# Keys and values of one batch kept for both parities, and position tables from one pattern

## The chip, the cores and the metric

One core of one Trainium2 chip runs the kernel. The metric is the device time of one execution in microseconds (us). The kernel before takes 676.55 us, the median of three runs (675.37 to 677.56). PE is TensorE, DVE VectorE, ACT ScalarE, POOL GpSimd, SP SyncE, which issues nearly all transfers.

## The reference

Attention with sinks and a sliding window, then a mixing block of low rank and a feed-forward net:

```
B, H, S, D = 4, 8, 768, 64        # n_sink = 4, window = 128
keep = (pos_k < n_sink) | ((pos_q - pos_k >= 0) & (pos_q - pos_k < window))
a = softmax(where(keep, q @ k.T / sqrt(D), -1e9));  x = a @ v    # heads joined: (B, S, 512)
h = x.transpose(0, 2, 1) @ U @ V                                 # U: 768x32, V: 32x768, float64
u = x + h.transpose(0, 2, 1)
out = u + relu(u @ w_ch1) @ w_ch2                                # 512 -> 2048 -> 512, float64
```

q, k and v are float32; U, V and both weight matrices arrive as float64 and are narrowed on the chip (`narrow`, seven or so small operations for each block on DVE, ACT and POOL).

## The kernel before

**Work and order.** Every operation is a step of a planner (`Plan`, line 293). A step has a modelled duration on each engine that could do it, the steps that it must follow and a priority. `order` runs a greedy list schedule forward and backward for 40 rounds, keeps the one of least modelled cost, and the steps are then written out in that order: each engine executes its own list in order, SP's list of transfers too. Operations ahead of the main program (lines 1620 to 1650) are outside the plan; the narrowing of U, V and the first weight block is in the plan, without its loads, so the plan takes these as present at its start.

**Start.** Eight products of zeros wake PE. SP loads the two scalars (n_sink and window), keys of two pairs, U, V in two parts and a weight block. `Masks.__init__` (line 173) builds four tables of distances, 128 x 132 each, with POOL's iota and some fifteen DVE operations. `values` (line 155) turns the scalars into a flag with five small DVE operations; all engines load the flag and branch (line 1651). `Masks.fill` (line 209) turns the tables into additive masks, before DVE's own branch. The main program is `Fast`; `General` is for other scalars and does not run.

**Attention of batch 0.** 768 positions are split into two parities of 64-row blocks, "half 0" and "half 1". `attention_halves` (line 859) does all four pairs of heads for half 0, then for half 1; for each, `load` (line 715) fetches queries, keys (`kp`, 128 x 792) and values (`vp`, 128 x 768), then come scores (PE, line 744), a fold and a masked reduction on DVE (lines 752, 757), the exponential on ACT (line 760), scaling, transposes (line 799), and value products (line 827). `kp`, `qp` and `vp` are rings of NRAW = 3 tiles: a load waits until the third load before it has been read. Queries are loaded by half; keys and values are the same for both halves and loaded twice. The other batches do both halves at once, in the shadow of the feed-forward net.

**Mixing and feed-forward.** When both halves are done, `mix_end` forms the mixed input, and `ffn` (line 1024) runs batch 0 (first product at line 1046). `weights` (line 679) narrows pairs of weight blocks into NSLOT = 3 slots of two tiles (`w0` to `w5`, 8 KB of each partition). `join` (`nt`) is scratch of the narrowing, cleared once on POOL (line 1647) and first needed by line 142. `shrink` and `stage` reuse rings and weight tiles later.

Of the kernel before, what the change touches and what calls it, by code (L numbers as in the profile page):

```python
# [21 lines left out]
P = 128  # L22
B, H, S, D = 4, 8, 768, 64
NB = S // P
# [145 lines left out]
class Masks:  # L170


    def __init__(self, nc, pool):
        self.nc, self.work = nc, pool
        raw = pool.tile([P, 4, SW], I32, name="mask")
        self.m = m = f32(raw)
        self.now, self.past = (pool.tile([P, G], I32, name=x) for x in ("now", "past"))
        two = lambda x: x.rearrange("p k (s c) -> p k s c", s=2)
        nc.gpsimd.iota(two(raw[:, 0:2, :P]), [[0, 2], [G, 2], [-1, G]], base=0, channel_multiplier=1)
        nc.gpsimd.iota(two(raw[:, 2:4, NS:]), [[0, 2], [-G, 2], [-1, G]], base=G, channel_multiplier=1)  # L180
        nc.gpsimd.iota(raw[:, 0:2, P:], [[4 * P, 2], [-1, NS]], base=0, channel_multiplier=1)
        nc.gpsimd.iota(raw[:, 2:4, :NS], [[4 * P, 2], [-1, NS]], base=G, channel_multiplier=1)
        cix = pool.tile([P, 4, NS], I32, name="m_cix")
        nc.gpsimd.iota(cix, [[0, 4], [1, NS]], base=0, channel_multiplier=0)
        self.cix = f32(cix)
        flat = lambda x: x.rearrange("p a b -> p (a b)")
        nc.vector.tensor_copy(flat(self.m), flat(raw))
        nc.vector.tensor_copy(self.cix, cix)
        v = nc.vector
        lo, hi = slice(0, G), slice(G, P)  # L190
        v.tensor_scalar(flat(m[hi]), flat(m[hi]), -float(G), None, ALU.add)
        far = pool.tile([P, 2, G], F32, name="m_far")
        back = m[:, 1, :G]
        v.tensor_scalar(self.now, back, 0.0, None, ALU.is_ge)
        v.tensor_scalar(self.past, back, 0.0, None, ALU.is_lt)
        v.tensor_scalar(far[:, 1], back, 0.0, float(P), ALU.is_lt, ALU.mult)
        v.tensor_scalar(far[lo, 0], back[lo], 0.0, FAR, ALU.is_lt, ALU.mult)
        fold = lambda x: x.unsqueeze(1)
        for at in (m[:, 0:2, :G], m[:, 2:4, NS + G:]):
            v.tensor_tensor(at[hi], at[hi], far[hi, 1].unsqueeze(1).broadcast_to([G, 2, G]), ALU.add)  # L200
            v.tensor_tensor(at[lo], at[lo], far[lo], ALU.add)
        nc.gpsimd.memset(m[lo, 0, G:P], FAR)
        sinks = m[lo, 0, P:]
        v.tensor_scalar(far[lo, 0, :NS], sinks, 0.0, FAR, ALU.is_lt, ALU.mult)
        v.tensor_tensor(sinks, sinks, far[lo, 0, :NS], ALU.add)
        for sinks in (m[hi, 0, P:], m[hi, 2, :NS]):
            v.tensor_scalar(sinks, sinks, float(P), None, ALU.add)

    def fill(self, ns, w):
        nc, m = self.nc, self.m  # L210
        ck = self.work.tile([P, 4, NS], F32, name="m_ck")
        nc.vector.tensor_scalar(ck, self.cix, ns, None, ALU.is_lt)
        sinks = (m[:, 0:2, P:], ck[:, 0:2]), (m[:, 2:4, :NS], ck[:, 2:4])
        for x, c in sinks:
            nc.vector.scalar_tensor_tensor(c, x, w, c, ALU.is_ge, ALU.mult)
        rows = m.rearrange("p a b -> p (a b)")
        nc.vector.tensor_scalar(rows, rows, w, -NEG, ALU.is_ge, ALU.mult)
        for x, c in sinks:
            nc.vector.tensor_scalar(x, c, NEG, NEG, ALU.mult, ALU.subtract)
# [334 lines left out]
class Fast:  # L554
# [21 lines left out]

    def fixed(self, n, shape, dtype, name):

        ring = Ring(n, None)

        def get(view=lambda t: t):
            return ring(lambda i=len(ring.boxes) % n: view(self.place(name, i, shape, dtype)))
        get.ring, get.name = ring, name
        return get
# [94 lines left out]
    def weights(self, f, prio):  # L679

        i, n = f // 2, 2 * P
        old = self.used.pop(0) if len(self.pairs) >= NSLOT else None
        slot = self.home[i] = len(self.pairs) if old is None else self.home[old]
        ws = self.pairs[i] = [Box(lambda layer=layer: self.wtiles[2 * slot + layer],
                                  () if old is None else (self.pairs[old][layer],)) for layer in range(2)]
        four = lambda x: x.rearrange("p (q j) -> p q j", q=4)
        for layer, src in enumerate((self.w1, self.w2)):
            w, wd, sums = ws[layer], self.wd[layer][i], self.ws[layer][i]
            for d in range(2):
                at = prio + 4.2 * d + 2.0 * layer  # L690
                tb, tw = self.narrow(src[f + d], DM, at, self.flat())
                hi, lo = (lambda d=d, w=w, o=o: w()[:, d, :, o:o + P] for o in (0, P))
                self.copy(DM, hi, lambda tw=tw: four(tw()), r=(tb,), w=((w, (d, 0)),), prio=at)
                self.tt(DM, lo, lambda tw=tw: four(tw()), lambda hi=hi: f32(hi()), ALU.subtract,
                        r=(tb, (w, (d, 0))), w=((w, (d, 1)),), prio=at)
                self.put(wd, lambda w=w, wd=wd, d=d: (f32(wd())[:, d], f32(w())[:, d, :3]), 3 << 17, at,
                         r=((w, (d, 0)), (w, (d, 1))), part=d)
                if i in LATER[layer]:
                    box = self.fd[layer][i][d]
                    self.put(box, lambda box=box, tw=tw: (box(), tw()), 1 << 18, at, r=(tb,))  # L700
                else:
                    self.prepare(tb, tw, sums, d, prio + 8.0)
        return ws
# [11 lines left out]
    def load(self, b, pair, half, t0):  # L715

        q0, q1 = (0, S) if half is None else (half * CH, (half + 1) * CH)
        kr, qr = self.kp(), self.qp()
        if b > 0 or half > 0 or pair >= NFIRST:
            self.put(kr, lambda: (kr(), self.k[b, pair]), NB * SW * 512, t0 - 16)  # L720
            self.put(qr, lambda: (qr()[:, :q1 - q0], self.q[b, pair][:, q0:q1]), (q1 - q0) * 512, t0 - 15)
        vr = self.vp()
        self.put(vr, lambda: (vr(), self.v[b, pair]), NB * 65536, t0 - 8)
        return (qr, q0), kr, vr
# [403 lines left out]
    def stage(self, bigs, nts):  # L1128
# [3 lines left out]
        wt = lambda i, n, o: ((self.pairs[self.used[i // 2]][i % 2],), lambda: self.wtiles[  # L1132
            2 * self.home[self.used[i // 2]] + i % 2].rearrange("p a b c -> p (a b c)")[:, o:o + n])
# [219 lines left out]
    def run(self):  # L1353
# [13 lines left out]
        self.wtiles, self.banks, self.bigs, self.accs = [], [], list(self.early), []  # L1367
# [20 lines left out]
        self.vp = fixed(NRAW, [P, 2, NB, D], F32, "vp")  # L1388
        self.p = fixed(NP, [P, 2, NBLK, SW], F32, "p")
# [56 lines left out]
        self.wtiles += [self.pool.tile([P, 2, 4, 2 * P], F32R, name=f"w{i}") for i in range(2 * NSLOT)]  # L1446
# [167 lines left out]
def sink_attention_mixer(ctx, tc, q, k, v, vs, limits, U, V, w1, w2, out):  # L1614
# [5 lines left out]
    with tc.tile_pool(name="idle", bufs=1, space=PSUM) as idle, tc.manual_schedule():  # L1620
# [18 lines left out]
        masks = Masks(nc, sp)  # L1639
# [6 lines left out]
        join = pre.tile([P, NNT, DM], I32, name="nt")  # L1646
        nc.gpsimd.memset(join, 0)
        ns, w, flag = values()
        rv = nc.values_load(flag[0:1, 0:1], min_val=0, max_val=1)
        masks.fill(ns, w)  # L1650
    with tc.If(rv > 0) as cmp:
# [76 lines left out]
```

## Time and profile before

| | |
|---|---|
| median of three runs | 676.55 us |
| profiled execution, its own time | 676.41 us |
| its span, first to last instruction | 674.60 us |
| busy: PE / DVE / ACT / POOL | 651.0 / 531.9 / 429.6 / 246.1 us |
| transfers | 194.70 MB, mean 289 GB/s |
| mean granted clock of PE | 0.993 of full speed |

Busy time is the time in which an engine executes instructions; PE is busy for 97% of the span. The share is a mean over stages with different limits, so stretches are read apart. An engine's list in order of time shows each instruction's start and length and, in brackets, how long the engine was idle before it and what ended that idle time.

### The profile page before, as it was taken

The numbers are of one execution on the slowest core, as the hardware profiler recorded it, in microseconds if no ns is written. First come the engines' busy times: TensorE is split into PE (matmuls) and PEld (weight loads), VectorE is DVE, ScalarE is ACT, GpSimd is POOL, SyncE is SP. The second block draws the span as 40 slices with busy tenths as digits, with TensorE's granted clock in tenths as the row PEclk, the third lists the DMA queues.
The fourth block names the chain that finished last, engine by engine and source line by source line (L and its number), as shares of the span: only waits on it lengthen the run. The fifth ranks groups of instructions, "written<-read, shape, count | busy, mean of one in ns | idle before, by whom it ended". The sixth has DMA issues, their size and how long they took to land.

```text
span 674.6 us, 14574 instructions
## 1 busy us (share of the span) xinstructions
PE 651.0 (97%) x4822; PEld 601.5 (89%) x4822; DVE 531.9 (79%) x1504; ACT 429.6 (64%) x1187; POOL 246.1 (36%) x297
## 2 busy tenths in 40 slices
PE   4988999999999999999999999999999999999997
PEld 3766888888899989898889899999999999999996
DVE  7898998999998987889799789746736964673483
ACT  5987589799585378756588976344437535543551
POOL 3564454346424346338264572110303211020120
PEclk9899999999999999999999999999999999999999
DMA  8869999999788799997899866899788899888883
GB/s 310 274 223 338 331 367 357 344 287 351 276 300 311 252 342 357 363 309 245 277 294 362 280 184 209 263 356 310 243 260 252 271 296 357 270 246 260 252 262 105
DMA packets 135252, 194.70 MB, mean 289 GB/s; under 512 B 10368, under 2 KB 103936, under 8 KB 135168
## 3 DMA queue, kind: packets, MB, share of 16 engines
q1 hardware_dynamic: 134880, 193.29, 85.8%
q8 instruction: 40, 0.66, 0.4%
q10 hardware_dynamic: 288, 0.39, 0.2%
q14 instruction: 44, 0.36, 0.2%
HBM read 144.36 MB, written 49.28 MB: 287 GB/s over the span
## 4 chain that ended last, share of the span: by engine, by line
PE 84%; DVE 8%; ACT 3%; DMA 2%; issue 1%; POOL 1%; POOLq 0%; ACTq 0%; DVEq 0%
PE bank L1212 48%; PE bank L1068 10%; PE bank L827 5%; PE bank L744 4%; PE bank L1046 3%; PE bank L1048 3%; PE bank L1047 3%; PE bank L799 3%; DMA w<-ws 2%; PE bank L933 1%; ACT p L760 1%; DVE p L757 1%; PE bank L942 1%; PE bank L956 1%; DVE nt L142 1%
## 5 line engine op out<-in xcount | busy, mean ns | idle before, releaser
L1212 PE MATMUL bank<-w,w 128*128 128x384 f32 x678 | 130.7, 337 | 0.4 <-DMA w<-ws 0.3
L1212 PEld LDWEIGHTS bank<-w,w 128*128 128x128 f32 x678 | 118.4, 188 | 2.8 <-issue 0.9
L760 ACT ACTIVATE p<-p,mn 128x132 f32<-128x132 f32 x192 | 75.7, 399 | 12.8 <-DVE mn L757 12.8
L630 POOL TENSOR_TENSOR w<-uh,w 128x384 fp32r<-128x384 f32 x24 | 25.5, 1063 | 145.6 <-ACT w L621 80.2
L1212 PE MATMUL bank<-w,spare 128*128 128x384 f32 x342 | 65.2, 335 | 0.0
L1217 DVE TENSOR_TENSOR big<-bank,big 128x384 f32<-128x384 f32 x84 | 44.7, 554 | 24.9 <-PE bank L1212 21.6
L630 POOL TENSOR_TENSOR spare<-spare 128x128 f32<-128x128 f32 (+1 forms) x54 | 42.1, 788 | 52.8 <-DMA ws<-spare 21.9
L1068 PE MATMUL bank<-w,hh 128*128 128x512 f32 x192 | 61.3, 400 | 0.0
L1212 PEld LDWEIGHTS bank<-w,spare 128*128 128x128 f32 x342 | 60.1, 188 | 0.0
L757 DVE CUSTOM_DVE_ANT_0 p<-bank,mask 128x132 f32<-128x132 f32 x192 | 47.9, 288 | 0.1
L744 PE MATMUL bank<-kp,qp 64*64 64x196 f32 (+4 forms) x896 | 43.3, 325 | 2.6 <-DVE sc_flag L165 2.6
L827 PEld LDWEIGHTS bank<-oph,vp 128*64 128x64 f32 x768 | 40.3, 137 | 5.5 <-issue 2.1
L1046 PE MATMUL bank<-ul,w 128*128 128x384 f32 x128 | 44.2, 345 | 0.7 <-POOL ul L630 0.7
L807 POOL TENSOR_SCALAR_AFFINE_SELECT oph<-oph 128x384 f32<-128x384 f32 x64 | 35.8, 572 | 23.9 <-ACT oph L621 19.8
L621 ACT CAST w<-uh 128x384 fp32r<-128x384 f32 x58 | 29.8, 514 | 21.5 <-PE bank L1212 19.9
L1048 PE MATMUL bank<-uh,w 128*128 128x384 f32 x128 | 43.2, 337 | 0.0
L1047 PE MATMUL bank<-uh,w 128*128 128x384 f32 x128 | 43.1, 337 | 0.0
L827 PE MATMUL bank<-oph,vp 128*64 128x128 f32 (+1 forms) x768 | 42.9, 266 | 0.1
L1212 PE MATMUL bank<-spare,w 128*128 128x384 f32 x204 | 41.7, 339 | 0.2 <-DVE ul L1217 0.2
L1068 PEld LDWEIGHTS bank<-w,hh 128*128 128x128 f32 x192 | 34.7, 188 | 6.4 <-issue 1.1
L744 PEld LDWEIGHTS bank<-kp,qp 64*64 64x64 f32 x896 | 30.0, 139 | 11.4 <-issue 6.6
L621 ACT CAST w<-ul 128x384 fp32r<-128x384 f32 x53 | 27.3, 515 | 19.2 <-PE bank L1212 18.5
(274 smaller groups left out, 1680.5 us busy)
## 6 DMA issues: line engine op xcount, KB each, us to landing
w<-ws SPq DMA_DIRECT2D x132, 256.0 KB, 4.2
w<-wd SPq DMA_DIRECT2D x102, 256.0 KB, 4.5
big<-in_w_dram SPq DMA_DIRECT2D x32, 512.0 KB, 5.7
ws<-spare SPq DMA_DIRECT2D x32, 512.0 KB, 5.3
spare<-ws SPq DMA_DIRECT2D x60, 256.0 KB, 4.0
wd<-w SPq DMA_DIRECT2D x32, 384.0 KB, 5.8
spare<-wd SPq DMA_DIRECT2D x42, 256.0 KB, 4.2
vp<-in_v_dram SPq DMA_DIRECT2D x20, 384.0 KB, 5.4
```

Of the source, the lines that this page charges most:

```text
L621: return self.plan.any({"ACT": (act(n) + (0.0 if psum else 0.07), lambda: nc.scalar.copy(dst(), src()), False), "DVE": (dve(n) if psum els ...
L630: ways["POOL"] = (gps(n), lambda: nc.gpsimd.tensor_tensor(dst(), a(), b(), op), True)
L744: nc.tensor.matmul(st()[a * G:(a + 1) * G, x * TW + to:x * TW + to + wd], qr()[at, q0:q0 + G], kr()[at, k0:k0 + wd], start=True, stop=True ...
L757: add("DVE", dve(SW), lambda st=st, x=x, j=j, part=part, at=at: nc.vector.tensor_tensor_reduce(part(), st()[:, x * TW + half * G:x * TW + ...
L760: add("ACT", act(SW) + 0.22, lambda part=part, at=at: nc.scalar.activation(part(), part(), AF.Exp, bias=at(mn), scale=-1.0, accum_out=at(sm)),
L827: nc.tensor.matmul(pa()[i * D:(i + 1) * D, kb * G:kb * G + hi - lo], vr()[:, i, kb, :], mv, start=kb == 0, stop=kb == NB - 1, skip_group_c ...
L1046: nc.tensor.matmul(ph()[:, :CH], wh, ul()[:, c, :], start=n == 0, stop=False)
L1047: nc.tensor.matmul(ph()[:, :CH], wl, uh()[:, c, :], start=False, stop=False)
L1048: nc.tensor.matmul(ph()[:, :CH], wh, uh()[:, c, :], start=False, stop=n == NC - 1)
L1068: nc.tensor.matmul(acc[k](), a()[:, sl], w()[:, :, at, m:m + P].rearrange("p d o j -> p o d j"), start=not begin and i == 0 and j == 0, st ...
L1212: nc.tensor.matmul(bank()[:, :CH], w()[:, at:at + P], u()[:, d, :] if n > 1 else u(), start=first and i == 1, stop=last and i == 3 * n, sk ...
L1217: add("DVE", dve(CH), lambda: nc.vector.tensor_tensor(x(), bank()[:, :CH], t(), ALU.add), r=(bank,) if t is x else (bank, t), w=(x,), prio ...
```

## The change

`Masks` builds one 128 x 128 pattern (and a small sink pattern) with POOL and eight DVE operations, in scratch room that is the `join` tile; `fill` makes one mask block on DVE and copies the others from it with seven ACT instructions. The clearing of `join` moves behind `fill`. For batch 0 `load` fetches keys and values only in half 0 and keeps them: pairs 0 to 2 in the three ring tiles, pair 3 in the room of the third weight slot (`w4`, `w5`), whose first block must wait for the last reader of that pair. Weight tiles are made when first used.

```diff
@@ -170,53 +170,44 @@
...
+    def __init__(self, nc, pool, room):
...
+        self.m = pool.tile([P, 4, SW], F32, name="mask")
...
+        raw, self.t = (x.rearrange("p (a b) -> p a b", b=G) for x in (room[:, 0, :2 * G], f32(room)[:, 1, :3 * G]))
+        sinks, self.cix = (pool.tile([P, n, NS], I32, name=x) for x, n in (("m_sink", 2), ("m_cix", 1)))
+        self.s = pool.tile([P, 2, NS], F32, name="m_s")
+        nc.gpsimd.iota(raw, [[-G, 2], [-1, G]], base=P, channel_multiplier=1)
+        nc.gpsimd.iota(sinks, [[G, 2], [-1, NS]], base=0, channel_multiplier=1)
+        nc.gpsimd.iota(self.cix, [[0, 1], [1, NS]], base=0, channel_multiplier=0)
+        v, t = nc.vector, self.t
+        self.lo, self.hi = lo, hi = slice(0, G), slice(G, P)
+        nc.gpsimd.memset(self.m[lo, 0, G:P], -NEG)
+        v.tensor_copy(t[lo, 0:2], raw[lo])
+        v.tensor_scalar(t[hi, 0:2], raw[hi], -float(G), None, ALU.add)
+        v.tensor_scalar(self.now, t[:, 1], float(G), None, ALU.is_ge)
+        v.tensor_scalar(self.past, t[:, 1], float(G), None, ALU.is_lt)
+        v.scalar_tensor_tensor(t[:, 0], self.now, -float(P), t[:, 0], ALU.mult, ALU.add)
+        v.scalar_tensor_tensor(t[lo, 2], self.past[lo], FAR, t[lo, 0], ALU.mult, ALU.add)
+        v.tensor_copy(self.s[lo], sinks[lo].bitcast(U32))
+        v.tensor_scalar(self.s[hi], sinks[hi].bitcast(U32), float(G), None, ALU.add)
     def fill(self, ns, w):
...
+        nc, m, t, lo, hi = self.nc, self.m, self.t, self.lo, self.hi
+        v, copy = nc.vector, nc.scalar.copy
+        ck = self.work.tile([P, 3, NS], F32, name="m_ck")
+        v.tensor_scalar(ck[:, 2], self.cix[:, 0], ns, None, ALU.is_lt)
+        v.scalar_tensor_tensor(ck[:, 0:2], self.s, w, ck[:, 2].unsqueeze(1).broadcast_to([P, 2, NS]), ALU.is_ge, ALU.mult)
+        rows = lambda x: x.rearrange("p a b -> p (a b)")
+        for part, at, src in ((slice(0, P), (1, slice(0, P)), rows(t[:, 0:2])), (hi, (0, slice(0, P)), rows(t[hi, 0:2])),
+                              (lo, (0, slice(0, G)), t[lo, 2])):
+            v.tensor_scalar(m[part, at[0], at[1]], src, w[part], -NEG, ALU.is_ge, ALU.mult)
+        two = lambda x: x.unsqueeze(1).broadcast_to([P, 2, G])
+        for k, at, c in ((0, P, 0), (1, P, 2), (2, 0, 1), (3, 0, 2)):
+            nc.scalar.activation(m[:, k, at:at + NS], ck[:, c], AF.Copy, bias=-NEG, scale=NEG)
+        copy(m[:, 2:4, NS:NS + G], two(m[:, 1, G:P]))
+        copy(m[:, 2:4, NS + G:], two(m[:, 1, :G]))
+        copy(m[lo, 2, NS + G:], m[lo, 0, :G])
@@ -574,6 +565,11 @@
+    def wtile(self, i):
+        if i not in self.wtiles:
+            self.wtiles[i] = self.pool.tile([P, 2, 4, 2 * P], F32R, name=f"w{i}", tag=f"w{i}", bufs=1)
+        return self.wtiles[i]
+
     def fixed(self, n, shape, dtype, name):
@@ -681,8 +677,9 @@
-        ws = self.pairs[i] = [Box(lambda layer=layer: self.wtiles[2 * slot + layer],
-                                  () if old is None else (self.pairs[old][layer],)) for layer in range(2)]
+        ws = self.pairs[i] = [Box(lambda layer=layer: self.wtile(2 * slot + layer),
+                                  (self.pairs[old][layer],) if old is not None else (self.extra[layer],) if slot == NSLOT - 1 else ())
+                              for layer in range(2)]
@@ -715,13 +712,17 @@
     def load(self, b, pair, half, t0):
-        kr, qr = self.kp(), self.qp()
-        if b > 0 or half > 0 or pair >= NFIRST:
-            self.put(kr, lambda: (kr(), self.k[b, pair]), NB * SW * 512, t0 - 16)
+        qr, early = self.qp(), b == 0 and half == 0 and pair < NFIRST
+        if half != 1:
+            extra = b == 0 and pair >= NRAW
+            kr, vr = self.keys[pair] = (self.spare_k(), self.spare_v()) if extra else (self.kp(), self.vp())
+            if not early:
+                self.put(kr, lambda: (kr(), self.k[b, pair]), NB * SW * 512, t0 - 16)
+        if not early:
-        vr = self.vp()
-        self.put(vr, lambda: (vr(), self.v[b, pair]), NB * 65536, t0 - 8)
-        return (qr, q0), kr, vr
+        if half != 1:
+            self.put(vr, lambda: (vr(), self.v[b, pair]), NB * 65536, t0 - 8)
+        return (qr, q0), *self.keys[pair]
     def scores(self, half, js, t0, q, kr, row):
@@ -1129,8 +1130,8 @@
-        wt = lambda i, n, o: ((self.pairs[self.used[i // 2]][i % 2],), lambda: self.wtiles[
-            2 * self.home[self.used[i // 2]] + i % 2].rearrange("p a b c -> p (a b c)")[:, o:o + n])
+        wt = lambda i, n, o: ((self.pairs[self.used[i // 2]][i % 2],), lambda: self.wtile(
+            2 * self.home[self.used[i // 2]] + i % 2).rearrange("p a b c -> p (a b c)")[:, o:o + n])
@@ -1364,7 +1365,7 @@
-        self.wtiles, self.banks, self.bigs, self.accs = [], [], list(self.early), []
+        self.wtiles, self.banks, self.bigs, self.accs = {}, [], list(self.early), []
@@ -1386,6 +1387,10 @@
+        self.keys, self.extra = {}, []
+        for i, shape in enumerate(([P, NB * SW], [P, 2, NB, D])):
+            self.extra.append(Box(lambda i=2 * NSLOT - 2 + i, shape=shape: self.pool.tile(shape, F32, name=f"own{i}", tag=f"w{i}", bufs=1)))
+        self.spare_k, self.spare_v = (lambda box=box: box for box in self.extra)
@@ -1443,7 +1448,6 @@
-        self.wtiles += [self.pool.tile([P, 2, 4, 2 * P], F32R, name=f"w{i}") for i in range(2 * NSLOT)]
         with tc.manual_schedule():
@@ -1636,18 +1640,18 @@
-        masks = Masks(nc, sp)
+        join = pre.tile([P, NNT, DM], I32, name="nt")
+        masks = Masks(nc, sp, join)
-        join = pre.tile([P, NNT, DM], I32, name="nt")
-        nc.gpsimd.memset(join, 0)
         masks.fill(ns, w)
+        nc.gpsimd.memset(join, 0)
```

## Rows read from the trace of the kernel before

**Rows 1.** Stretch, us; PE, PEld, DVE, ACT, POOL busy (instructions); PE clock, DMA share, GB/s.

```profile
9.20:66.70 57.50, 45.97 (x522) 35.15 (x516) 51.93 (x212) 48.36 (x174) 28.48 (x40) 0.94 0.85 293
...
66.70:670.30 603.60, 599.28 (x4260) 560.98 (x4260) 474.33 (x1267) 379.08 (x1011) 213.95 (x241) 1.00 0.88 291
```

**Rows 2.** PE in order of time: start us, us, what, [idle before <-releaser].

```profile
7.18 3.70 PE L744 MATMUL bank<-kp,qp 64*64 64x128 f32 x56 [2.58 <-DVE sc_flag L165]
...
51.41 2.64 PE L827 MATMUL bank<-oph,vp 128*64 128x128 f32 x48
...
66.75 0.44 PE L1046 MATMUL bank<-ul,w 128*128 128x384 f32 x1 [0.67 <-POOL ul L630]
```

**Rows 3.** DVE in order of time, start of the execution.

```profile
1.77 0.43 DVE L187 CAST mask<-mask 128x528 f32<-128x528 int32 x1 [1.77 <-POOL mask L182]
...
5.42 0.16 DVE L157 SCALAR_TENSOR_TENSOR sc_t<-sc_raw 128x2 f32<-128x2 int32 x1
...
6.07 0.22 DVE L165 SCALAR_TENSOR_TENSOR sc_flag<-sc_c,sc_val 128x1 int32<-128x1 f32 x1
6.96 0.34 DVE L212 TENSOR_SCALAR m_ck<-m_cix,sc_val 128x16 f32<-128x16 f32 x1 [0.68 <-DVE sc_flag L165]
...
8.35 0.25 DVE L219 TENSOR_SCALAR mask<-m_ck 128x8 f32<-128x8 f32 x2
9.22 0.36 DVE L136 TENSOR_SCALAR nr<-big 128x384 uint16<-128x384 uint16 x1 [0.63 <-DMA big<-in_V_dram]
...
10.66 0.48 DVE L752 COPY_PREDICATED bank<-now,bank 128x128 f32<-128x128 int32 x2
```

**Rows 4.** ACT in order of time.

```profile
8.16 0.38 ACT L137 ACTIVATE nr<-big 128x192 bf16<-128x192 bf16 x1 [5.87 <-DMA big<-in_U_dram]
...
9.15 0.56 ACT L138 ACTIVATE big<-big 128x384 int32<-128x384 uint32 x1 [0.34 <-DMA big<-in_V_dram]
...
17.95 0.21 ACT L787 COPY psink<-p 128x24 f32<-128x24 f32 x1
...
19.31 0.48 ACT L621 COPY oph<-bank 128x384 f32<-128x384 f32 x1 [0.58 <-DVE oph L803]
```

**Rows 5.** DMA issues: out<-in engine op xcount, KB each, median us to landing.

```profile
vp<-in_v_dram SPq DMA_DIRECT2D x20, 384.0 KB, 5.4
kp<-in_k_dram SPq DMA_DIRECT2D x18, 396.0 KB, 5.7
...
sc_raw<-in_limits_dram SPq DMA_DIRECT2D x1, 2.0 KB, 3.7
```

**Rows 6.** SP's issues in order of time.

```profile
0.81 0.40 SPq L151 DMA_DIRECT2D sc_raw<-in_limits_dram  x1
...
6.58 0.33 SPq L1638 DMA_DIRECT2D big<-in_w_dram  x1
...
11.76 0.33 SPq L636 DMA_DIRECT2D kp<-in_k_dram  x1
...
25.22 0.33 SPq L636 DMA_DIRECT2D kp<-in_k_dram  x1
...
28.10 4.22 SPq L636 DMA_DIRECT2D vp<-in_v_dram  x2
...
43.66 0.33 SPq L636 DMA_DIRECT2D vp<-in_v_dram  x1
...
71.72 0.33 SPq L636 DMA_DIRECT2D big<-in_w_dram  x1
```

**Rows 7.** POOL in order of time.

```profile
3.66 0.95 POOL L1647 MEMSET nt<- 128x1024 int32 x1
```

**Rows 8.** Busy time of the stretch from 30 us to the first feed-forward product.

```profile
30.00:66.75 36.75, 32.29 (x312) 24.38 (x310) 32.22 (x101) 29.27 (x94) 20.18 (x27) 1.00 0.77 260
```

**Rows 9.** DVE by line, 9.2 to 66.7 us: operation xcount | busy, mean ns | idle.

```profile
L757 DVE CUSTOM_DVE_ANT_0 p<-bank,mask 128x132 f32<-128x132 f32 x48 | 12.2, 288 | 0.1
...
L752 DVE COPY_PREDICATED bank<-past,bank 128x128 f32<-128x128 int32 (+1 forms) x16 | 3.6, 256 | 0.0
```

More of the change, by code (lines that the diff above doesn't have):

```diff
@@ L170 @@
 class Masks:
-    def __init__(self, nc, pool):
+    def __init__(self, nc, pool, room):
         self.nc, self.work = nc, pool
-        raw = pool.tile([P, 4, SW], I32, name="mask")
-        self.m = m = f32(raw)
+        self.m = pool.tile([P, 4, SW], F32, name="mask")
         self.now, self.past = (pool.tile([P, G], I32, name=x) for x in ("now", "past"))
[L178 to L207, printed above, removed]
@@ L209, in fill @@
-    def fill(self, ns, w):
[L210 to L219, printed above, removed]
+        raw, self.t = (x.rearrange("p (a b) -> p a b", b=G) for x in (room[:, 0, :2 * G], f32(room)[:, 1, :3 * G]))
```

## The prediction

> **What bounds the kernel now.** I read the table of stretches first, then PE's, DVE's, ACT's and SP's instructions in order of time, then the DMA issues. The profiled execution took 676.41 us, of which 674.60 are the span and 1.81 lie around it; the median of the three runs is 676.55, so a change of the span is carried over one to one, plus 0.14.
>
> PE divides the span in two. From its first feed-forward product at 66.75 [rows 2] to 670.3 PE's matmuls are busy 599.28 of 603.60 us [rows 1]: 4.3 us of idle in all. What that part costs is its work, which the change leaves as it is. So the time follows the moment at which the first product starts, and the gaps, which are small. Before that moment PE works 45.97 of 57.50 us, while DVE works 51.93 and ACT 48.36 [rows 1]: attention of batch 0, the preparation of U and V and the first weights go through DVE and ACT, and DVE's idle time is 57.50 - 51.93 = 5.57 us. This stage is where a gain must be made.
>
> How does DVE get into the stage? The masks are finished at 8.35 + 0.25 = 8.60 [rows 3]. Then DVE stands idle for 0.63 us, until 9.22, and what ends that is not an engine but the transfer of V's first half [rows 3]. Behind this instruction, in DVE's fixed order, stand the other U and V conversions, and only at 10.66 the first operation on scores [rows 3], though PE began them at 7.18 [rows 2]. ACT too starts with a transfer: U at 8.16 after 5.87 us of idle, V at 9.15 [rows 4]. The start of the main program is therefore tied to the arrival of U and V, not to the masks.
>
> **The masks, before the flag.** Removed are the wide table operations on DVE between 1.77 and 5.42 [rows 3]; in their place come eight small ones. Their durations are not in the trace. The nearest rows are 0.16 us (a 128x2 operation) and 0.43 us (the 128x528 cast) [rows 3], so eight take 1.3 to 3.4 us; I take 0.2 each, nearer to the small row, 1.6 in all, from about 1.5 to 3.1 us. But the scalars that the flag needs were issued at 0.81 [rows 6] and land 3.7 us later [rows 5], at 4.5. From there to the flag it is 5.42 to 6.29, 0.87 us [rows 3]. So the flag is ready at about 5.4 (with the dear end, 1.77 + 3.4 + 0.87 = 6.0) instead of 6.29: 0.9 us earlier at best, although some 2 us of DVE work are gone. What is late next is the scalars' transfer.
>
> **The masks, after the flag.** DVE starts the filling 0.67 us after the flag [rows 3], now at 6.1. Five operations on 128x4 to 128x128 elements stand against five that took from 6.96 to 8.60 with one of 528 columns: I take 0.24 each, 1.2 us, to 7.3. ACT gets seven new instructions ahead of its first conversion, four of 4 columns and three of 64 to 128. The nearest rows are 0.21 us (24 columns) and 0.48 us (384) [rows 4]: 1.5 to 3.4 us together; I take 4 x 0.21 + 3 x 0.28 = 1.7, as most are near the small row. They can't begin before DVE's second filling operation, at about 6.7, and end at 8.4 (dear end: 10.1). U's conversion started at 8.16, so ACT slips by 0.2 us; but V, at 9.15, is the next thing for which ACT waits, after 0.34 us of idle [rows 4], and there the slip is gone. The cover fails where the ACT copies end after some 8.5: then each further tenth delays V's conversion by as much, up to about 1.3 us at the dear end.
>
> The Trainium skill, ScalarE: Activation LUTs, section "What ACT_TABLE_LOAD costs", states that an activation with immediate scale and bias costs 186 ns and 0.833 ns per column, and that neighbours overlap by about 93 ns. By that the seven copies are an estimated 4 x 0.19 + 2 x 0.29 + 0.24 - 6 x 0.093 = 1.0 us, and end at 7.7, ahead of U; no row here shows a copy of these widths, and the sum below does without it.
>
> The clearing of the join tile on POOL, 0.95 us at 3.66 [rows 7], moves behind the filling, as its room is scratch now: 7.3 to 8.3. DVE first needs it behind the V conversion of 9.22, so it is hidden; if the filling were over only at 9, up to 0.7 us would be seen.
>
> So DVE reaches its first main instruction at 7.3 instead of 8.6, and finds V missing until 9.15 to 9.2 as before: SP issued U, V and the first weight block ahead of the flag, and that is unchanged. The gain of this part is 0, with its cover named: V's transfer. If the order on DVE were to change so that score work stands ahead of V, up to 9.2 - 7.5 = 1.7 us of work would move ahead of the wait.
>
> **The loads.** Removed are eight transfers of the second parity: four of keys, issued between 11.76 and 25.22, and four of values, between 28.10 and 43.66 [rows 6], 396 and 384 KB each [rows 5], 3.1 MB. They lie on the DMA rings beside attention, and no PE, DVE or ACT instruction of that stage is shown to wait for one. From 30 on the rings are filled only to 0.77 [rows 8]. SP loses eight issues, but the raw weight blocks that stand among them wait for buffers that DVE has to free, and DVE isn't faster. Value: 0; nearest bounds are 0 and the one idle time that DVE has for an early DMA, 0.63 us.
>
> What is added: keys and values of the fourth pair lie in the room of the third weight slot, which must wait until they have been read. The last reader is the value product from 51.41 to 54.05 [rows 2]; the ninth raw weight block, the first for that slot (the eight before it were issued from 6.58 on), is issued only at 71.72 [rows 6]. 17 us of room: 0.
>
> **The order.** A planner writes out the order of all engines from modelled durations; fewer loads, and keys that don't wait for a ring, give it another problem, and so another order everywhere. This term has no row of its own. It is bounded on the good side by DVE's idle time before 66.75, 5.57 us, on the bad side by one row of scores (six 128x132 blocks of one pair and parity) done ahead of more urgent work: 12.2/8 for its reductions and 3.6/4 for its folds [rows 9], 2.4 us of DVE. Fewer constraints lean to the good side; I take a sixth of the idle time, -0.9 us, because DVE's and ACT's work in the stage is the same and nothing that made them idle there is touched. Sum: 0 + 0 + 0 - 0.9, that is 675.5 for the profiled execution, 675.6 against the median.
>
> **Rivals.**
> A, the forecast: 675.6, own range 674.6 to 677.5; chance 0.44.
> B, the start moves. The new order puts scores ahead of V's conversions on DVE (1.7 us), and some 1.6 of the 5.57 us of idle time go as half 1 has its keys at hand: -3.3, 673.2. For it speaks that DVE and ACT are short of nothing but time until 66.75, so an earlier start is kept. Against it: U and V count as present from the planner's first moment, while scores need PE first, so its greedy rule starts DVE with U and V again. Chance 0.33, since either half alone already passes the bound below when the other helps a little.
> C, slower. Place: DVE between 20 and 58, where it has no reserve. Without a key transfer the second parity's scores are ready sooner, and a row of them runs ahead of the transposed sums that the mixing matrix waits for: +2.4 us at the first feed-forward product, 679.0. It decides from the point at which a row is taken ahead of one of the last blocks of half 0 or of the weight preparation for the first product. Against it: all rows must be done before 66.75 anyway. Chance 0.14.
> D, ACT's copies reach beyond V's arrival: +1.3 at the dear end, 677.8; chance 0.05.
> E, the saving is not what it says: the third weight slot is wanted earlier in the new order and its blocks wait for the fourth pair's values. It costs from the point at which that slot's preparation moves from 72 to before 54; a weight block late by a PE row of some 2.5 us gives 679.0. Chance 0.04.
>
> **From the cases to the numbers.** 0.3%, about what a measurement of this kernel tells from no change, is 2.0 us: 674.5 to 678.6. A and D lie inside (0.49), B below (0.33), C and E above (0.18). The likeliest is A, 675.6. The range takes B with a further 1.2 us of its idle time, to 672.0, and C to 679.0.
>
> **What would show it.** The flag near 5.4, PE's scores near 6.3, masks full on DVE by 7.3 and on ACT by 8.4; DVE's idle time ahead of its first V or U conversion grown from 0.63 to nearly 2 us, still ended by a DMA: then the mask part was hidden, as said. If instead DVE's first main instruction is a fold of scores well before 9, B is right. The first feed-forward product tells the sum: 65.8 in A, 63.5 in B, 69 in C. Keys and values of batch 0 must be issued eight times less. The prediction is wrong in kind if PE's idle time after the first product moves by more than 1.5 us from 4.3: then the order of the later stages, which I cost at nothing, decides.

## The result and the profile after

The changed kernel takes 679.74 us (median of 5 runs, 679.42 to 681.61) against 675.88 (5 runs, 675.37 to 677.56): ratio 1.0057, 95% interval [1.0038, 1.0077], 3.9 us slower. A second measurement beside later experiments gave 679.72 and 1.0045 [1.0031, 1.0059]. The profiled execution is the longest of the first five, with a span of 679.9 us; the other four have 677.7 to 678.0, so waits that appear in it are also looked up in the second profile (span 678.5).

The table of stretches of the kernel after; columns as in [rows 1]:

```profile
9.20:66.70 57.50, 47.88 (x508) 35.43 (x501) 50.14 (x216) 49.23 (x177) 26.36 (x38) 0.91 0.69 236
66.70:670.00 603.30, 596.06 (x4235) 556.27 (x4236) 469.77 (x1244) 380.83 (x1018) 220.54 (x257) 1.00 0.87 290
```

The loss lies in the second row. PE's idle time there is 603.30 - 596.06 = 7.24 us, and its last matmul ends at 674.71, behind this stretch. [rows 1] give 4.32, but their stretch goes on behind the last matmul of the kernel before, at 669.57; up to there PE is idle for 3.53 us. The first stage, in which I looked for a gain, starts the first feed-forward product at the same time as before in this profile, 66.70 against 66.75 in [rows 2]. The second profile has it at 65.92, and four more of this order, one with the old masks and three with single instructions moved, at 65.94 to 66.28. PE's granted clock was 0.50, its level of 1.2 GHz, until 24 us in the first profile and until 21 in the second.

VectorE in order of time, kernel after: first the start, which answers to [rows 3], then three places of the later stages.

```profile
4.54 0.16 DVE L157 SCALAR_TENSOR_TENSOR sc_t<-sc_raw 128x2 f32<-128x2 int32 x1 [1.67 <-DMA sc_raw<-in_limits_dram]
...
5.18 0.22 DVE L165 SCALAR_TENSOR_TENSOR sc_flag<-sc_c,sc_val 128x1 int32<-128x1 f32 x1
...
6.48 0.86 DVE L204 TENSOR_SCALAR mask<-nt,sc_val 128x128 f32<-128x128 f32 x3
9.21 0.36 DVE L136 TENSOR_SCALAR nr<-big 128x384 uint16<-128x384 uint16 x1 [1.87 <-DMA big<-in_V_dram]
...
10.65 0.48 DVE L753 COPY_PREDICATED bank<-now,bank 128x128 f32<-128x128 int32 x2
...
85.06 1.50 DVE L618 CAST w<-spare 128x512 fp32r<-128x512 f32 x1
86.49 0.28 DVE L140 TENSOR_SCALAR nr<-nr 128x512 uint16<-128x512 uint16 x1
86.69 0.55 DVE L1058 SCALAR_TENSOR_TENSOR hl<-bank,hh 128x384 fp32r<-128x384 f32 x1
...
312.37 1.82 DVE L624 TENSOR_TENSOR uh<-uh 128x384 f32<-128x384 f32 x2
314.11 0.54 DVE L618 COPY pair384b<-psink 128x384 f32<-128x384 f32 x1
...
353.53 0.78 DVE L618 CAST vsh<-pair512a 128x512 fp32r<-128x512 f32 x1 [0.93 <-DMA pair512a<-in_vs_dram]
354.34 0.69 DVE L997 TENSOR_TENSOR t<-bank,t 32x512 fp32r<-32x512 f32 x1
```

The flag is ready at 5.40, the masks at 7.34, and then DVE waits 1.87 us for V where it waited 0.63. It converts V at 9.21 and folds its first scores at 10.65, to 0.01 us as in [rows 3].

ScalarE, kernel after: the end of its mask copies and U, which answer to [rows 4], then a place after the first product.

```profile
7.51 0.24 ACT L210 COPY mask<-mask 64x64 f32<-64x64 f32 x1
8.16 0.38 ACT L137 ACTIVATE nr<-big 128x192 bf16<-128x192 bf16 x1 [0.41 <-DMA big<-in_U_dram]
...
72.99 0.66 ACT L138 ACTIVATE spare<-big 128x512 int32<-128x512 uint32 x1 [2.25 <-DMA big<-in_w_dram]
...
74.10 0.47 ACT L1055 ACTIVATE hh<-bank 128x384 fp32r<-128x384 f32 x1
```

PE, kernel after: its first product and its four longest idle places behind it; then the first product of the run below that has the same order without the new masks.

```profile
66.70 0.44 PE L1047 MATMUL bank<-ul,w 128*128 128x384 f32 x1 [0.69 <-POOL ul L626]
...
74.62 0.73 PE L1069 MATMUL bank<-w,hh 128*128 128x512 f32 x2 [0.76 <-ACT hh L1055]
...
87.29 0.44 PE L1047 MATMUL bank<-ul,w 128*128 128x384 f32 x1 [1.12 <-DVE hl L1058]
...
314.70 0.55 PE L904 MATMUL bank<-ident,pair384b 128*128 128x128 f32 x3 [1.46 <-DVE pair384b L618]
...
355.08 0.62 PE L1010 MATMUL bank<-vst,t 128*128 128x384 f32 x2 [1.54 <-DVE t L997]
```

```profile
66.12 0.45 PE L1056 MATMUL bank<-ul,w 128*128 128x384 f32 x1 [0.68 <-POOL ul L635]
```

SP's queue ahead of the first of these places, kernel after, then the kernel before:

```profile
59.79 0.52 SPq L632 DMA_DIRECT2D xd<-xg  x1
...
65.16 0.32 SPq L632 DMA_DIRECT2D kp<-xd  x1
...
66.53 0.37 SPq L632 DMA_DIRECT2D big<-in_w_dram  x1
```

```profile
63.37 0.33 SPq L636 DMA_DIRECT2D big<-in_w_dram  x1
...
65.18 0.41 SPq L636 DMA_DIRECT2D kp<-xd  x1
```

Read together, the four engines tell one story per place. At 74.62 PE waits for ScalarE's hh. ScalarE was free, but ahead of hh in its queue stood the copy of a raw weight block (72.99) that had not landed for 2.25 us. The block had not landed because SP issued it only at 66.53, behind the read back of xd (65.16), which follows 4.9 us behind the issue of the last store that it reads (59.79 + 0.52). It is the eighth block from the start; in the kernel before, SP issues the eighth at 63.37, ahead of the read back at 65.18. At 87.29 PE waits for hl, ahead of which DVE had a cast of 1.50 us and a scaling. At 355.08 PE waits for t, and ahead of t in DVE's queue stands a cast that waits 0.93 us for its own transfer. At 314.70 it waits for a copy behind two subtractions of 1.82 us. Each is an instruction that stands in an in-order queue behind a late or long one that it doesn't need. In the second profile the four places measure 0.44, 1.13, 1.45 and 0.38 us.

### The profile page after: what moved, and what is told of

Same layout as the page of the kernel before. It is cut to its first block, busy times and chain, and to the rows that moved or that the text cites. A ratio compares the mean times of both kernels' runs of the same rounds, so it can differ in the third digit from the quotient of the medians.

```text
span 679.9 us, 14610 instructions
## 1 busy us (share of the span) xinstructions
PE 655.3 (96%) x4822; PEld 602.3 (89%) x4822; DVE 525.6 (77%) x1481; ACT 433.4 (64%) x1205; POOL 249.9 (37%) x309
## 4 chain that ended last, share of the span: by engine, by line
PE 76%; DVE 13%; ACT 5%; DMA 2%; issue 1%; DVEq 0%; ACTq 0%
PE bank L1213 48%; PE bank L1069 7%; PE bank L828 5%; PE bank L745 4%; PE bank L1047 2%; PE bank L1049 2%; PE bank L1048 2%; PE bank L800 2%; ACT p L761 2%; PE bank L934 1%; DVE w L624 1%; DVE p L758 1%; DVE nt L142 1%; DMA big<-in_w_dram 1%; DMA pair512a<-in_vs_dram 1%
## 5 line engine op out<-in xcount | busy, mean ns | idle before, releaser
L626 POOL TENSOR_TENSOR spare<-spare 128x128 f32<-128x128 f32 (+1 forms) x61 | 39.7, 663 | 34.5 <-DMA ws<-spare 19.8
L745 PE MATMUL bank<-kp,qp 64*64 64x196 f32 (+2 forms) x840 | 40.8, 329 | 1.7 <-DMA kp<-in_k_dram 1.7
L828 PEld LDWEIGHTS bank<-oph,vp 128*64 128x64 f32 x720 | 37.7, 137 | 5.1 <-issue 3.7
L617 ACT CAST w<-ul 128x384 fp32r<-128x384 f32 x57 | 29.3, 517 | 19.5 <-PE bank L1213 17.8
L617 ACT COPY nt<-bank 128x384 f32<-128x384 f32 x34 | 16.1, 476 | 38.9 <-PE bank L1213 37.7
L828 PE MATMUL bank<-oph,vp 128*64 128x128 f32 x720 | 40.2, 267 | 0.0
```

What stands on the lines that cost most here:

```text
L617: return self.plan.any({"ACT": (act(n) + (0.0 if psum else 0.07), lambda: nc.scalar.copy(dst(), src()), False), "DVE": (dve(n) if psum els ...
L626: ways["POOL"] = (gps(n), lambda: nc.gpsimd.tensor_tensor(dst(), a(), b(), op), True)
L745: nc.tensor.matmul(st()[a * G:(a + 1) * G, x * TW + to:x * TW + to + wd], qr()[at, q0:q0 + G], kr()[at, k0:k0 + wd], start=True, stop=True ...
L828: nc.tensor.matmul(pa()[i * D:(i + 1) * D, kb * G:kb * G + hi - lo], vr()[:, i, kb, :], mv, start=kb == 0, stop=kb == NB - 1, skip_group_c ...
```

## The experiments

The theory formed from this: neither part of the change costs or gives anything; the planner's search ends with another order, and that order holds more such waits. Rivals: the masks cost; the kept tiles or the third weight slot cost; the idle places are only symptoms.

**One part at a time.** The first run adds the new masks to the kernel before and no other line. The second takes the old masks into the changed kernel.

```diff
-        masks = Masks(nc, sp)
+        join = pre.tile([P, NNT, DM], I32, name="nt")
+        masks = Masks(nc, sp, join)
```

> The kernel before with the new masks alone; keys and values are loaded twice as before, and the planner's order is the one of before. Theory 1 (the new order costs the time; the masks are hidden behind the transfer of V): 675.9, ratio 0.998 to 1.002; flag at 5.4, DVE's first main instruction still at 9.2, first feed-forward product at 66.7. Theory 2 (seven more ACT instructions and the later clearing of the join tile cost something that shows downstream): 677 to 680.

> The changed kernel with the old masks: keys and values stay on the chip, and the planner's order is that of the changed kernel. Theory 1 (the order): 679.7, ratio 1.004 to 1.008, with PE idle at the same four places after the first feed-forward product (near 74.6, 87.3, 314.7 and 355.1). Theory 2 (the masks): 675.9.

The masks alone: 676.17, ratio 0.9999 [0.9990, 1.0007]. The change without its masks: 678.8, 1.0038 [1.0025, 1.0051], just under the 1.004 expected. The masks are free, and the loss comes with the kept keys and values, which are the part that the planner sees. Its idle places are not quite the four expected: 0.73 us at 85.1 and 1.47 at 312.6 are there, 0.44 is left at 352.5, and near 74 there is none of 0.3 us or more.

**The kept tiles in the order of before.** The planner still counts all loads and so finds the order of before, but the eight repeated transfers are not issued and the tiles are kept. The first run has the old masks, the second both parts of the change.

```diff
-            d, s = pair()
-            self.nc.sync.dma_start(d, s)
+            x = pair()
+            if x is not None:
+                self.nc.sync.dma_start(*x)
...
-            self.put(kr, lambda: (kr(), self.k[b, pair]), NB * SW * 512, t0 - 16)
+            self.put(kr, lambda: None if kept and half else (kr(), self.k[b, pair]), NB * SW * 512, t0 - 16)
```

> Keys and values stay on the chip and the eight transfers are not issued, but the planner solves the problem of before (with the eight loads and the rings as they were), so every engine's order is that of before; old masks. Theory 1 (the order alone): 675.9, ratio 0.997 to 1.002, PE idle after 66.7 near 4.0 us as before. Theory 3 (keeping the tiles itself costs: their place in the third weight slot, or the other traffic): 679 to 680, whatever the order. If the eight transfers had been in the way of something: 673 to 675.

> Both parts of the change (the tiles kept, eight transfers not issued, the new position tables), with the order of the kernel before. Theory (only the order costs): 676 to 677, ratio 0.999 to 1.002, TensorE idle some 4 us after 66.7 us at the places of the kernel before. Rival (the two parts harm each other, by ScalarE's seven copies or the third weight slot, whatever the order): 679 or more.

They took 676.86, 1.0010 [1.0001, 1.0019], and 676.91, 1.0003 [0.9994, 1.0012]. The second does all that the change does, and is as fast as the kernel before; the changed kernel beside it took 679.72. Its row after 66.7 us:

```profile
66.70:670.00 603.30, 599.40 (x4260) 561.57 (x4260) 473.71 (x1266) 379.57 (x1010) 216.85 (x241) 1.00 0.88 291
```

PE's idle time is 3.90 us. So the order makes the loss, whatever is kept, and 3.1 MB fewer transfers are worth nothing that can be told. The order here includes the engine, which the plan chooses for many operations: from 9.2 us on the changed kernel has 1463 instructions on DVE, 1194 on ScalarE and 294 on GpSimd, the kernel before 1478, 1183 and 280.

**The cover of the masks.** U and V's first half are issued ahead of pair 1's keys, in the order of before with both parts of the change. This takes away the wait that hid the faster masks.

```diff
+            for src, n in sources[:2] if h == 0 else sources[2:]:
+                early.append(pre.tile([P, RAW], I32, name=f"big{len(early)}"))
+                nc.sync.dma_start(early[-1].bitcast(U16)[:, 1:4 * n + 1], src)
```

> The order of before, keys and values kept, the new masks, and U and the first half of V issued ahead of the second pair's keys. It tries whether the transfer of V was what covered the masks. If so, V lands some 0.4 MB of traffic earlier, near 8.2 instead of 9.15, DVE's first main instruction starts with it, and as DVE is the engine that is short until 66.7 the whole moves by about 1 us: first feed-forward product near 65.7, time 674.9, ratio 0.997 to 1.000. If the start is held by something else (the second pair's scores, which get their keys later): DVE starts early but the first product stays at 66.7, 675.9.

It took 676.1, 0.9998 [0.9989, 1.0006]. DVE, PE, the stretch to 20 us and the microsecond from 21 of this run:

```profile
8.15 0.36 DVE L136 TENSOR_SCALAR nr<-big 128x384 uint16<-128x384 uint16 x1 [1.11 <-DMA big<-in_V_dram]
...
9.59 0.48 DVE L758 COPY_PREDICATED bank<-now,bank 128x128 f32<-128x128 int32 x2
```

```profile
8.56 2.26 PE L750 MATMUL bank<-kp,qp 64*64 64x128 f32 x28 [1.33 <-DMA kp<-in_k_dram]
16.14 1.68 PE L805 MATMUL bank<-ident,p 128*128 128x128 f32 x6 [5.32 <-POOL p L787]
...
22.88 1.31 PE L833 MATMUL bank<-oph,vp 128*64 128x128 f32 x20
```

```profile
9.20:20.00 10.80, 5.48 (x59) 3.51 (x54) 9.96 (x52) 9.48 (x39) 3.30 (x4) 0.50 0.99 362
...
21.00:22.00 1.00, 1.00 (x13) 0.67 (x15) 0.95 (x6) 1.00 (x6) 0.29 (x1) 0.50 0.80 266
```

PE and the same microsecond in the kernel before:

```profile
16.99 1.54 PE L799 MATMUL bank<-ident,p 128*128 128x128 f32 x6 [6.12 <-POOL p L781]
...
22.54 1.43 PE L827 MATMUL bank<-oph,vp 128*64 128x128 f32 x24
```

```profile
21.00:22.00 1.00, 1.00 (x25) 0.83 (x26) 1.00 (x10) 1.00 (x5) 0.54 (x1) 1.00 0.89 320
```

V's conversion and the first fold came 1.07 us earlier, the first product only 0.26 (66.49), between the two expectations and nearer to the second. The scores of pair 1 now wait 1.33 us for their keys, but they end at 10.82, where the kernel before ends them at 10.88, and PE's next work, the transposes, starts 0.85 us earlier (16.14 against 16.99). This lead is lost at half speed: PE's granted clock stays at 0.50 until 22 us, where the kernel before is back at full speed behind 20, with 13 matmuls from 21 to 22 against 25. The value products start 0.34 us later than before (22.88 against 22.54). Both parts in the old order without V first have 0.50 until 22 us as well, and their first product at 66.72. So V's transfer was the cover, as the prediction says, and by these rows most of the lead that it hid goes into PE's longer stretch at half speed.

**How far orders scatter.** One longer search of the changed problem, its second-best order, and the second and third best of the unchanged problem. No computation differs, only the order.

```diff
-ROUNDS = 40
+ROUNDS = 200
...
-        for s, p in zip(self.steps, best[1]):
+        for s, p in zip(self.steps, sorted(tried)[PICK][2]):
```

> The changed kernel with the planner's search run for 200 rounds instead of 40, so that it ends with another order, the best that it finds. Theory 1 (which order the search happens to end with decides, and orders of one problem scatter by several us): anything between 674 and 681, with PE idle after the first feed-forward product at other places than those of the changed kernel. Theory 4 (a problem without the eight loads leads to slower orders as such): 679 to 681, with idle of 6 us or more.

> The changed kernel with the planner's second best order of its 40 rounds in place of the best. Theory 1: scatter, 674 to 681, other places of idle. Theory 4: 679 to 681.

> The kernel before with the planner's second best order of its 40 rounds; nothing else is changed, keys and values are loaded twice. Theory 1: as scattered as the changed kernel's, 674 to 681, likely 1 to 4 us slower than 676.1, as the best was chosen. Theory 4: 675 to 677.

> The kernel before with the planner's third best order. Theory 1: 674 to 681, likely 1 to 4 us slower than 676.1. Theory 4: 675 to 677.

| order | us | ratio to before | first product | PE idle, 66.7 to 670 |
|---|---|---|---|---|
| changed, longer search | 678.53 | 1.0027 [1.0013, 1.0042] | 64.35 | 5.3 |
| changed, second best | 677.02 | 1.0012 [0.9998, 1.0025] | 64.83 | 5.1 |
| before, second best | 678.77 | 1.0016 [0.9999, 1.0033] | 64.95 | 6.5 |
| before, third best | 678.88 | 1.0051 [1.0030, 1.0071] | 66.36 | 6.8 |

The unchanged kernel in its third-best order is as slow as the changed one, and the changed one in its second-best order, 677.02, is below the 679 to 681 of theory 4: the new problem does not lead to slow orders as such. For before's second best the median and the ratio differ because its twelve executions spread from 674.8 to 679.5; its interval takes in 1. Three of the four start the first product 1.8 to 2.4 us earlier than the kernel before and are no faster, so that moment does not set the time. The planner's own cost does not rank orders: the longer search's has the lowest of all, 1325.94, and takes 678.53; the order of before costs 1326.64 and takes 676.68 beside it; the changed kernel's best and second best cost 1328.73 and 1328.78 and lie near 3 us apart. No order that was run is faster than that of before, and a change of the planner's input draws again.

**Single waits taken away.** In the written order of the changed kernel one instruction is moved (the weight block ahead of the read back), then a second (the cast behind t), then a third (the copy pair384b ahead of the subtractions). Beside the first two runs the changed kernel once more.

```diff
         order = self.plan.order()
+        moved = [s for s in order[at[first]:at[late]] if s in self.tags["back"]]
+        order = [s for s in order if s not in moved]
+        i = order.index(late) + 1
+        order[i:i] = moved
...
+        order.insert(order.index(low) + 1, cast)
...
+        order[i:i] = late + [rep]
```

> The changed kernel, one instruction moved: on SP's queue the weight block that ScalarE copies at 72.99 us is issued ahead of the pair of transposes read back from the stores, whose issue at 65.16 us waited for those stores to land. Theory (the loss after 66.7 us is made of waits behind late instructions in in-order queues): the block is issued near 63.4 us and lands near 69 to 70, ScalarE's wait of 2.25 us is gone, TensorE's idle 0.76 us at 74.6 is gone and the 1.12 at 87.3 shrinks: 0.8 to 1.9 us less than the changed kernel beside it, 678 to 679, ratio to before 1.002 to 1.005. Rival (the idle places are not the cause, what is lost returns elsewhere): within 0.5 us of the changed kernel.

> The move of the run above, and one more: on VectorE the cast of a shared-weight block that waited 0.93 us for its transfer at 353.5 us is put behind the instruction that TensorE waits for (the low part t of the batch in work). Theory: TensorE's idle 1.54 us at 355.1 goes as well, 2.3 to 3.4 us less than the changed kernel, 676.3 to 677.5, ratio to before 1.000 to 1.002. Rival (idle time returns elsewhere, because the next wait is just behind): under 1 us less than the changed kernel.

> The changed kernel itself, beside the two moves, as their reference: 679 to 680.5, ratio 1.004 to 1.008 by every theory.

> The changed kernel with the two moves, and a third: on VectorE the copy of the sink parts (pair384b, 0.54 us) that TensorE waited 1.46 us for at 312 us goes ahead of the two subtractions (1.82 us together) that stood before it though it needs neither; on ScalarE its fellow pair384a goes ahead of one cast. Theory (TensorE's idle places make the whole loss): idle at 312 falls from 1.46 to under 0.5, 1.0 to 1.5 us less than with two moves, ratio to before 0.999 to 1.001, 676 to 677. Rival (what is won by moves is given back at the places behind, and a floor of some +1.4 us belongs to the change itself): ratio 1.0015 to 1.003.

One move: 678.55, 1.0032 [1.0020, 1.0043], 1.2 us less than the 679.72 beside it; at 87.29 0.22 us of the idle 1.12 are left. Two moves: 678.03, 1.0020 [1.0011, 1.0029], 1.7 less, where 2.3 to 3.4 were expected. Three: 677.8, 1.0022 [1.0010, 1.0035]; the third gave nothing that can be told. The two places with two moves, on SP, ScalarE and DVE:

```profile
63.04 0.36 SPq L635 DMA_DIRECT2D big<-in_w_dram  x1
63.46 0.45 SPq L635 DMA_DIRECT2D kp<-xd  x1
```

```profile
70.02 0.66 ACT L138 ACTIVATE spare<-big 128x512 int32<-128x512 uint32 x1
```

```profile
349.56 0.69 DVE L1002 TENSOR_TENSOR t<-bank,t 32x512 fp32r<-32x512 f32 x1
350.28 0.43 DVE L621 CAST vsh<-pair512a 128x512 fp32r<-128x512 f32 x1
```

Both waits are gone. PE and ScalarE with three moves:

```profile
310.16 0.55 PE L910 MATMUL bank<-ident,pair384b 128*128 128x128 f32 x3
...
314.14 0.79 PE L923 MATMUL bank<-pst,vsh 128*128 128x384 f32 x3 [1.00 <-DVE pst L627]
```

```profile
311.82 0.88 ACT L620 COPY oph<-bank 128x384 f32<-128x384 f32 x2 [1.47 <-DVE oph L808]
...
313.01 0.48 ACT L620 CAST pst<-bank 128x384 fp32r<-128x384 f32 x1
```

The 1.46 us are gone, and 4 us later PE waits 1.00 us for pst. ScalarE makes its part of pst behind copies that wait for DVE, which had only been given the same work in another sequence. With two moves the same product ran without a wait, at 314.87: the first wait had covered this one. The expectation that the three places make up the loss is refuted: with three moves PE's idle rows are no longer than before's, and the kernel is still slower.

**The same in the kernel before.** Nothing of the change, two instructions moved on DVE.

```diff
+        for name, n in ("xT10", 3), ("xT21", 1):
...
+                order.insert(max(i, order.index(wait)), s)
```

> The kernel before, nothing of the change, two instructions moved on VectorE: the additions xT that TensorE waits for at 170.8 (0.97 us idle) go ahead of a scaling of a weight block (1.38 us), and the first of those at 321.7 (0.56 us idle) ahead of a subtraction of a weight block (1.43 us). Theory (orders are told apart by such waits alone): 0.9 to 1.5 us less, ratio 0.9977 to 0.999. Rival (the two long instructions run 1.4 us, where their like run 0.3 to 0.6, beside GpSimd's; moved, they stay long and hold up what is behind them, pst at 171.8 above all): within 0.3 us of before, ratio 0.9995 to 1.001.

It took 676.95, 1.0006 [0.9995, 1.0016]: the rival's ratio. PE of the kernel before, then DVE, ScalarE and PE of this run:

```profile
170.78 0.45 PE L916 MATMUL bank<-pst,vsh 128*128 128x384 f32 x1 [0.97 <-DVE xT L919]
```

```profile
169.14 1.48 DVE L922 TENSOR_TENSOR xT<-xT,bank 128x384 f32<-128x384 f32 x3
170.54 1.13 DVE L139 TENSOR_SCALAR nr<-nr 128x512 bf16<-128x512 bf16 x1
```

```profile
171.71 0.63 ACT L141 ACTIVATE nr<-nr 128x512 uint16<-128x512 uint16 x1 [1.83 <-DVE nr L139]
...
172.75 0.47 ACT L624 CAST pst<-bank 128x384 fp32r<-128x384 f32 x1
```

```profile
173.87 1.04 PE L919 MATMUL bank<-pst,vsh 128*128 128x384 f32 x4 [1.53 <-DVE pst L631]
```

PE no longer waits at 170.8 (0.97 us). But nr now comes later, ScalarE waits 1.83 us for it instead of 0.56, pst stands behind it in ScalarE's queue, and PE waits 1.53 us for pst. This profile also has a wait of 1.15 us for a transfer at 441.2, which the one before has not, and whether it belongs to the moves is not shown. No run here beats the kernel before by more than the measurement can tell.

**What the idle rows leave out.** From PE's rows, in us: the first product, the length from there to the end of the last matmul, the idle rows in it, and the rest.

| kernel | first | length | idle | rest |
|---|---|---|---|---|
| before | 66.75 | 602.82 | 3.53 | 599.28 |
| both parts, old order | 66.72 | 603.35 | 3.89 | 599.47 |
| changed, first profile | 66.70 | 608.01 | 7.24 | 600.77 |
| changed, second profile | 65.92 | 607.53 | 6.15 | 601.38 |
| two moves | 66.07 | 604.52 | 3.45 | 601.08 |
| three moves | 65.94 | 605.04 | 3.38 | 601.66 |

Between the first two rows and the changed order the idle rows differ by 2.3 to 3.7 us (without moves) and the rest by 1.3 to 2.1, over the same 4260 matmuls. The rest is time that the rows show as busy. A matmul of 384 columns has a row of 0.34 us while the next starts 0.17 us behind it, so a wait under 0.17 us leaves no idle row. The Trainium skill, Perfetto Trace Analysis, section "Tensor Engine Instruction (MATMUL, LD_WEIGHTS)", says that the end of a matmul is estimated rather than observed; these overlapping rows agree. Another sequence of shapes may also take longer by itself; no run separates the two. How the rest divides between short waits and the sequence stays open.

## Why the prediction was wrong

- **Masks before the flag:** right. Flag at 5.40 (5.4 forecast), the scalars' transfer now the last to arrive (4.54).
- **Masks after the flag:** right in the sum. DVE was full at 7.34 (7.3) and waited 1.87 us ("nearly 2"). ScalarE's copies ended at 7.75, where my rows gave 8.4: I had priced seven copies without their overlap (together they took 1.15 us from 6.60), and U was not delayed. The estimate from the Trainium skill, ScalarE: Activation LUTs, section "What ACT_TABLE_LOAD costs", 7.7, agrees with the trace. The gain of 0 is shown by the masks alone (0.9999), and the cover by V issued first: DVE's first conversion then came 1.07 us earlier.
- **Loads and third slot, 0:** right, 1.0003 with both parts in the old order. The late weight block of rival E's kind was late by SP's queue, not by its slot: a move on SP's queue alone freed it.
- **The order, -0.9, bounded by +2.4 and -5.57: this is the step that failed.** It measures +3.1 to +3.9. I bounded it by the stage before 66.75 alone and took the rest of the kernel as work that the change leaves as it is, with the time following the moment of the first product. In its own stage the term nearly came: the first product started 0.05 us earlier in the first profile and 0.83 in the second, though a sixth of the idle time was a guess, so this is luck. What I put at nothing is the order behind it: from the first product to the last matmul PE took 4.7 to 5.2 us longer, 2.6 to 3.7 of them idle and the others in rows that show it busy. The 4260 matmuls are the same; their order, and the order and in part the engine of what feeds them, are not. The clause on what would make the forecast wrong in kind, PE's idle time moving by more than 1.5 us, is what happened: 7.24 and 6.15 against 3.53. (The 4.3 named there has 0.74 us in it that lie behind the last matmul.)
- **Rivals:** B did not come: V's conversion still stands ahead of the first fold, and the first product is at 66.70 and 65.92, not 63.5. Where other orders start it at 64.4 to 65.0, the time is not shorter. C had the size of the loss but not its place: the first product is not late, and the late instructions are a weight block, two casts and a copy after 66.7. D did not come; its dear end, 10.1 against 8.5, would be 1.6 us, not 1.3.
- **The sign:** "fewer constraints lean to the good side" had no row behind it. The other orders that were run lie at 1.0006 to 1.0057, none below the one of before, though three of them can't be told from it. That a redraw from an order that happens to be a good one leans to the bad side is argued from these few. The planner's cost, though it ranks orders badly, leaned the other way ahead of any run: 1328.73 for the changed kernel against 1326.64, the sum of two modelled times, each about 1 us longer. Neighbouring orders of the kernel before differ by up to 0.51%, 3.4 us, and no term of the forecast had that scatter.

## What to carry to other kernels

Where a search writes the order, any edit of its input draws a new order of everything, so compare an edit under the old order too, and price the redraw by running a few neighbouring orders of the unchanged kernel: here +0.16%, not clear of noise, and +0.51%. An earlier start of the bounding stage proves nothing about the end. When PE waits, look at what stands ahead of the late instruction in its own queue, and at what that waits for; here one root was a load behind the read back of a store. A single wait taken away is worth its idle time only up to the next one behind it: 1.46 us freed gave back 1.00 four microseconds later, 0.97 gave 1.53.

## What the runs showed of the hardware

With V issued first, PE stood idle 1.33 us before 8.56, and its granted clock was 0.73 from 8 to 9 us and 0.50, the 1.2 GHz level, from 9 to 22. In the kernel before PE was idle from 10.88 to 16.99, and the clock was 0.50 from 14 to 20. The gap before 8.56 is not needed for a clock that stays down until 22: both parts in the old order have no gap from 6.12 to 8.40, are idle from there to 16.81, and stand at 0.50 from 12 to 22 too. At 0.50 the 28 score products of pair 1 took 2.26 us (8.56); those of pair 0, at 1.00, took 1.24 (5.98). The kernel before took 3.70 us for all 56 at a recorded 1.00, so the recorded clock is not the whole of it. No run here tells why the clock rises at 20 in one and at 22 in the others.

DVE's scaling nr, 128x512, takes 0.29 us at 167.94 of the kernel before and 1.38 us at 168.76, where GpSimd's operation on a weight block runs from 168.61 to 169.99; the additions xT beside GpSimd's next one take 0.55 us each, as they do elsewhere. The Trainium skill, SBUF — State Buffer, section "SBUF: two separate sides", says that VectorE and GpSimd share one port pair under an exclusive lock. The end of nr at 170.14, 0.15 us behind 169.99, agrees. Moved behind the additions, nr ran from 170.54 to 171.67, 0.15 us behind the end of the GpSimd operation that ran from 170.23 to 171.52.

```profile
167.94 0.29 DVE L139 TENSOR_SCALAR nr<-nr 128x512 bf16<-128x512 bf16 x1
...
168.76 1.38 DVE L139 TENSOR_SCALAR nr<-nr 128x512 bf16<-128x512 bf16 x1
```

```profile
168.61 1.38 POOL L630 TENSOR_TENSOR w<-spare,w 128x512 fp32r<-128x512 f32 x1 [1.97 <-ACT w L621]
```
